# Batch 0's loads reordered, a third PSUM pair for its KV sums, an MLP bank taken early, and the last output tile in column halves: a change to a fused attention and MLP kernel

## The chip, the cores and the metric

The kernel runs on one core of one Trainium2 chip. The metric is the device time of one execution in microseconds (us), so lower is better. A chip has engines that run their own instruction streams: PE (TensorE, matmuls), PEld (its weight loads), DVE (VectorE), ACT (ScalarE), POOL (GpSimd) and SP (SyncE, which here only issues DMAs). "Span" below is the time from the first to the last instruction in one profiled execution; it is about 2 us less than the device time of the same execution.

A run is called slow where it is over 1.5% above the fastest of the same kernel, and fast otherwise. Ratios below are the mean time of one kernel's fast runs over that of the other's fast runs of the same rounds on the same chip, so they are not quite the ratio of the medians that are quoted beside them. The interval after a ratio is a 95% interval. "Faster" and "slower" mean by over 2%.

## The reference

Attention with random features (8 batches, 8 heads, 576 tokens, 64 dimensions, 128 features) feeds an MLP (4608 tokens, 512 to 2048 to 512).

```python
def _attn_ref(q, k, v, omega):
    scale = 1.0 / np.sqrt(np.sqrt(D))
    q_s, k_s = (q * scale, k * scale)
    def phi(x):
        proj = np.einsum('bhsd,md->bhsm', x, omega)
        h = proj - np.sum(x * x, axis=-1, keepdims=True) / 2.0
        h = h - np.max(h, axis=-1, keepdims=True)
        return np.exp(h) / np.sqrt(m)
    q_p, k_p = (phi(q_s), phi(k_s))
    kv = np.einsum('bhsm,bhsd->bhmd', k_p, v)
    z = np.sum(k_p, axis=2)
    num = np.einsum('bhsm,bhmd->bhsd', q_p, kv)
    den = np.einsum('bhsm,bhm->bhs', q_p, z)[..., None] + 1e-06
    return num / den

def _moe_ref(x, w_in, w_out):          # x: attention's output, 4608 x 512
    h = x @ w_in
    g = h * (1.0 / (1.0 + np.exp(-1.702 * h)))
    return g @ w_out
```

## The kernel before

The work is cut into 32 pairs of heads (4 to a batch) and 9 MLP blocks of 512 tokens. A pair passes through these steps; the names are those of the code.

- `ld`: k, q and v of the pair are loaded on POOL's DMA queue.
- `TK`, `TQ` (pairs 0 to 11, on PE) or `TD` (pairs 12 to 31, a DMA transpose on SP's queue, `qkT<-qk` in the profile): q and k are transposed.
- `K`, `Q` (PE) and `expK`, `expQ`, `expM` (ACT): projections and exponentials. `mx0`, `mx1`, `rec` (DVE) and `vp` (POOL or DVE) scale v.
- `KV` (PE), `kvs` (ACT), `ND` (PE), `rd` and `xm` (DVE): the KV sums, numerator and denominator, and their quotient.
- `X` and `evX` (pairs 0 to 7, PE and a copy) or `XD` (pairs 8 to 31, a DMA transpose on SP's queue, `xt<-xb`): the result is transposed for the MLP.

The MLP is `m1` (PE), `tanh` (ACT), `stt` (DVE), `m2` (PE), `store` (ACT) and `st` (output DMAs on SP's queue). MLP blocks start when their batches are done, so most of the attention runs in among the MLP's matmuls.

No instruction order is written out by hand: when the kernel is built, a list scheduler written in the kernel simulates all engines with a table of assumed durations, and emits each engine's instructions in the order that this simulation gives. Each engine's queue then runs strictly in that order, whatever the real durations are.

```python
ENGINES = {"K": {"P": 0.280}, "expK": {"A": 0.905}, "m1": {"P": 0.864}, ...
           "vp": {"G": 1.300, "D": 0.740}, "ld": {"G": 0.550},
           "TD": {"S": 2.1}, "XD": {"S": 1.2}, "st": {"S": 1.0}}          # G is POOL, S is SP
LOADS = [("k", 1), ("q", 1), ("k", 2), ("v", 1), ("q", 2), ("k", 3), ("v", 2), ("q", 3), ("v", 3)]
LOADS += [("wi", j) for j in range(4)]
...
    def kv_bank(o):                          # where a pair's KV sums go
        b = {"nd": nd["free"]}
        if o[1] < 4 and ("Q", 3) not in left:
            b["pq0"] = banks["pq"]["pq0"]
        return min(((t, x) for x, t in b.items() if t is not None), default=None)
...
            if st["m"] == 0:                 # the first MLP matmul waits for all of batch 0's banks
                if any(("Q", i) in left for i in range(4)):
                    return None
                t = max([t, banks["tr"]["tr1"], banks["pq"]["pq1"]])
...
        if kind == "ld":
            size = 2.90 if x[0] in ("wi", "wo") else 0.95      # assumed us of transfer
...
        def TD(i):
            t = qkp.tile([128, NS, 128], BF16, name="qkT", tag="qkT")
            nc.sync.dma_start_transpose(t[:], qk_t[i][:])
...
        def load_v(i, eng=nc.sync):
            t = stv.tile([128, NS, D], F32, name="v", tag="v")
            eng.dma_start(t[:], vv[i])
...
        for n, (o, eng) in enumerate(schedule(res)):
            emit(o, eng)
```

The softmax here doesn't subtract the row's maximum and nothing guards it: scores larger than these inputs give would overflow.

## Time and profile before

| | before |
|---|---|
| device time, median of 3 runs | 330.55 us (330.18 to 331.05) |
| span of the profiled execution | 535.4 us |
| granted PE clock in it | 0.559 |
| PE busy in it | 517.9 us, 97% |

The profiled execution and the timed ones are not in the same condition: the span is 1.6 times the time, because the PE clock that was granted was 0.559 of full speed. The page of the kernel before says so. Its first lines are the span and the busy time of each engine (us, share, instructions); the row PEclk gives the granted clock in tenths for 40 equal slices of the span; the last line divides the chain of work that ended last by engine.

```profile
span 535.4 us, 6610 instructions
PE 517.9 (97%) x2551; PEld 204.8 (38%) x2598; DVE 185.7 (35%) x342; ACT 196.3 (37%) x355; POOL 92.4 (17%) x161
...
PEclk7555555555555555555555555555555555555555
...
PE 95%; issue 2%; ACT 1%; DMA 1%; DVE 1%; SPq 0%; ACTq 0%
```

PE is 95% of the chain. In the timeline of the head (start in us, duration, engine, line, operation, tiles and shapes; in brackets the idle time before it and what ended it) the gaps that the change aims at are to be seen.

```profile
22.77 0.53 PE L528 MATMUL pqk<-vp,ke 64*128 64x65 bf16 x18
24.69 0.22 DVE L555 RECIPROCAL r<-pqk 128x10 f32<-128x10 f32 x1 [2.08 <-PE pqk L546]
26.98 0.65 ACT L435 ACTIVATE xt<-tr 128x576 bf16<-128x576 bf16 x1 [2.19 <-PE tr L573]
28.59 1.58 ACT L594 ACTIVATE th<-mo 128x512 bf16<-128x512 f32 x3 [0.95 <-PE mo L584]
```

Pair 3's KV sums start at 22.77 us, DVE stands idle for 2.08 us before it can go on, the last X copy of batch 0 starts at 26.98 us, and the first tanh of the MLP at 28.59 us.

SP's queue is where a reader would later have wished to look. In its timeline (start, time that the issue took, queue, line, operation, tiles, count) the first transposes of q and k of the kernel before stand at these times.

```profile
85.96 2.91 SPq L412 DMA_TRANSPOSE qkT<-qk  x2
94.91 1.24 SPq L412 DMA_TRANSPOSE qkT<-qk  x1
```

They are issued in 1.2 to 1.5 us each, and PE waits for none: the view of PE's waits (engine, tile and line, what it waited for, us in total, times, longest) has no line with `DMA qkT<-qk`. Its largest is this one.

```profile
PE mo L604 <- issue: 3.0, 13, 0.3
```

### The profile page before, as it was taken

How to read it: one execution, taken by the hardware profiler on the slowest of the kernel's cores; microseconds unless marked ns; L12 is line 12 of the kernel's file. 1: busy time of each engine (PE TensorE's matmuls, PEld its weight loads, DVE VectorE, ACT ScalarE, POOL GpSimd, SP SyncE). 2: the span in 40 equal slices, each digit the busy share in tenths (PEclk: the TensorE clock that was granted, in tenths of full speed). 3: DMA queues.
4: the chain of work that ended last, by engine and by line, in shares of the span. 5: the costliest groups of instructions: out<-in, count | busy, mean ns of one | idle time of the engine just before them, and what ended most of it. 6: DMA issues, size and time to landing. Idle time of an engine off the chain costs nothing.

```text
span 535.4 us, 6610 instructions
## 1 busy us (share of the span) xinstructions
PE 517.9 (97%) x2551; PEld 204.8 (38%) x2598; DVE 185.7 (35%) x342; ACT 196.3 (37%) x355; POOL 92.4 (17%) x161
## 2 busy tenths in 40 slices
PE   7999999999999999999999999999999999999996
PEld 3534344443443333434334333433333333333332
DVE  4655534643433423333333333323222222222200
ACT  5555525544543424343343333443222222222210
POOL 7527012333322212222112010000000000000000
PEclk7555555555555555555555555555555555555555
DMA  9999218466655353543355223211100001100011
GB/s 226 228 229 203 54 39 151 94 122 112 126 108 120 77 111 80 105 99 72 69 90 122 55 43 66 44 32 32 32 21 20 20 20 33 27 20 20 21 39 39
DMA packets 61807, 43.10 MB, mean 81 GB/s; under 512 B 42768, under 2 KB 54800, under 8 KB 61776
## 3 DMA queue, kind: packets, MB, share of 16 engines
q0 software_dynamic: 15632, 22.49, 21.5%
q1 hardware_dynamic: 46144, 20.20, 18.0%
q8 instruction: 20, 0.33, 0.3%
q14 instruction: 11, 0.09, 0.1%
HBM read 36.73 MB, written 9.44 MB: 86 GB/s over the span
## 4 chain that ended last, share of the span: by engine, by line
PE 95%; issue 2%; ACT 1%; DMA 1%; DVE 1%; SPq 0%; ACTq 0%
PE mo L584 41%; PE mo L604 40%; PE nd L546 3%; PE nd L528 3%; PE pqk L455 2%; PE pqk L484 2%; PE tr L423 1%; DMA qf<-in_q_dram 1%; PE tr L573 1%; PE tr L429 1%; PE tr L644 1%; PE nd L460 1%; DVE gT L598 1%; ACT th L594 0%; PE pq L484 0%
## 5 line engine op out<-in xcount | busy, mean ns | idle before, releaser
L584 PE MATMUL mo<-xt,win 128*128 128x512 bf16 x553 | 238.9, 577 | 4.4 <-issue 1.9
L604 PE MATMUL mo<-wout,gT 128*128 128x512 bf16 x555 | 238.3, 579 | 4.2 <-issue 3.0
L598 DVE SCALAR_TENSOR_TENSOR gT<-th,mo 128x512 bf16<-128x512 bf16 x144 | 98.7, 687 | 245.5 <-ACT th L594 245.4
L594 ACT ACTIVATE th<-mo 128x512 bf16<-128x512 f32 x144 | 85.8, 597 | 228.6 <-PE mo L584 219.4
L604 PEld LDWEIGHTS <-gT 128*128 128x128 bf16 x576 | 71.6, 129 | 127.8 <-issue 125.2
L584 PEld LDWEIGHTS <-win 128*128 128x128 bf16 x576 | 71.2, 129 | 126.1 <-issue 123.4
L516 POOL CAST vp<-em 128x9 bf16<-128x9 f32 x27 | 6.1, 225 | 260.4 <-DVE em L508 180.2
L617 ACT ACTIVATE osb<-mo 128x512 f32<-128x512 f32 x36 | 21.5, 597 | 46.9 <-PE mo L604 44.8
L473 ACT ACTIVATE ke<-pqk 128x1024 bf16<-128x1024 f32 x32 | 33.1, 1034 | 0.0
L493 ACT ACTIVATE qe<-pqk 128x1024 bf16<-128x1024 f32 x28 | 28.6, 1020 | 8.9 <-PE pqk L484 8.7
L517 POOL TENSOR_TENSOR vp<-v,em 128x576 bf16<-128x576 f32 x27 | 31.3, 1159 | 0.0
L546 PEld LDWEIGHTS <-qe 128*128 128x128 bf16 x320 | 20.6, 119 | 13.7 <-issue 10.9
L563 DVE TENSOR_TENSOR xb<-nd,r 128x640 bf16<-128x640 f32 x30 | 24.7, 823 | 0.9
L503 DVE TENSOR_REDUCE m<-hm 128x9 f32<-128x576 bf16 x32 | 24.0, 750 | 0.5
L528 PEld LDWEIGHTS <-ke 64*128 64x128 bf16 x576 | 16.2, 108 | 12.1 <-issue 5.2
L555 DVE RECIPROCAL r<-nd 128x10 f32<-128x10 f32 x30 | 6.5, 218 | 41.2 <-PE nd L546 23.1
L546 PE MATMUL nd<-kvs,qe 128*128 128x65 bf16 x300 | 20.5, 231 | 0.3
L394 POOL DMA_DIRECT2D v<-in_v_dram x31 | 18.2, 587 | 3.2 <-DMA qk<-in_q_dram 2.1
L499 DVE TENSOR_TENSOR hm<-ke 128x576 bf16<-128x576 bf16 x32 | 14.9, 466 | 10.7 <-ACT ke L473 10.7
L528 PE MATMUL nd<-vp,ke 64*128 64x65 bf16 x540 | 18.5, 222 | 0.0
L387 POOL DMA_DIRECT2D qk<-in_k_dram x31 | 17.2, 555 | 4.2 <-issue 1.7
L390 POOL DMA_DIRECT2D qk<-in_q_dram x31 | 17.1, 551 | 2.4 <-DMA win<-in_moe_w_in_dram 2.0
(55 smaller groups left out, 186.1 us busy)
## 6 DMA issues: line engine op xcount, KB each, us to landing
out_dram<-osb SPq DMA_DIRECT2D x72, 128.0 KB, 2.3
v<-in_v_dram POOLq DMA_DIRECT2D x31, 288.0 KB, 3.9
qk<-in_k_dram POOLq DMA_DIRECT2D x31, 144.0 KB, 4.1
qk<-in_q_dram POOLq DMA_DIRECT2D x31, 144.0 KB, 4.5
win<-in_moe_w_in_dram POOLq DMA_DIRECT2D x4, 512.0 KB, 10.3
wout<-in_moe_w_out_dram POOLq DMA_DIRECT2D x4, 512.0 KB, 9.9
xt<-xb SPq DMA_TRANSPOSE x24, 2.6
qkT<-qk SPq DMA_TRANSPOSE x20, 3.2
```

The lines of the kernel that those rows point to most:

```text
L473: nc.scalar.activation(out=st[i]["ke"][:, 1:9, :].rearrange("p (j e) f -> p e j f", e=2), in_=pk[:].rearrange("p e (j f) -> p e j f", f=12 ...
L493: nc.scalar.activation(out=dst, in_=src, func=AF.Exp, scale=SCALE)
L503: nc.vector.reduce_max(out=m[:], in_=st[i]["hm"][:], axis=AX.X)
L517: e.tensor_tensor(out=t[:, :, 0:64], in0=v_t[i][:], in1=em[:].unsqueeze(2).to_broadcast([128, NS, 64]), op=ALU.mult,)
L528: nc.tensor.matmul(nd[:, e, 0:65], lhsT=ke[64 * e : 64 * e + 64, s, :], rhs=t[64 * e : 64 * e + 64, s, :], start=(s == 0), stop=(s == NS - 1),
L546: nc.tensor.matmul(nd[:, e, g * 65 : (g + 1) * 65], lhsT=qe[i % NQE][:, e, g * 128 : (g + 1) * 128], rhs=t[:, e, :],)
L563: nc.vector.tensor_tensor(out=xb[:].rearrange("p g e d -> p e g d"), in0=v4[:, :, :, 0:64], in1=r[:].unsqueeze(3).to_broadcast([128, 2, NG ...
L584: nc.tensor.matmul(dst, lhsT=win[:, c, f * 128 : (f + 1) * 128], rhs=xt[c][:, n * 512 : (n + 1) * 512], start=(c == 0), stop=(c == NC_ - 1),)
L594: nc.scalar.activation(out=t[:], in_=src, func=AF.Tanh, scale=0.851)
L598: nc.vector.scalar_tensor_tensor(out=gts[n][:, f, :], in0=t[:], scalar=1.0, in1=src, op0=ALU.add, op1=ALU.mult)
L604: nc.tensor.matmul(dst, lhsT=gts[n][:, f, r * 128 : (r + 1) * 128], rhs=wout[:, f, :], start=(f == 0), stop=(f == NFC - 1),)
L617: nc.scalar.activation(out=o[:], in_=src, func=AF.Copy, scale=0.5)
```

## The change

The intent is to start the dense MLP earlier and to end it earlier.

- k and q of pairs 1 to 3 are loaded ahead of all v, and the transposes of a pair depend on free q/k buffers instead of on the KV sums three pairs back.
- KV sums of batch 0 may use a third PSUM pair, `pq1`, as well.
- The MLP's first bank is the second transpose bank, `tr1`; the other two are cut out of `pq1` when pair 3 is done. So only two groups, not three, begin in parts.
- The last output tile is computed, stored and sent in two halves of 256 columns.
- `vp` of pairs 0 and 3 is bound to DVE and of pairs 1 and 2 to POOL, and two of the scheduler's assumed transfer times are lowered.

```diff
-LOADS = [("k", 1), ("q", 1), ("k", 2), ("v", 1), ("q", 2), ("k", 3), ("v", 2), ("q", 3), ("v", 3)]
+LOADS = [("k", 1), ("q", 1), ("k", 2), ("q", 2), ("k", 3), ("q", 3), ("v", 1), ("v", 2), ("v", 3)]
...
+TILES = [4] * (NBLK - 1) + [5]
+def last(n, r):
+    return n == NBLK - 1 and r >= 3
...
-        deps["TK", i] = p("TK", i - 1) + p("KV", i - 3) + p("Q", i - 3) + l("k") + l("q")
+        deps["TK", i] = p("TK", i - 1) + p("K", i - NQK) + p("Q", i - NQK) + l("k") + l("q")
...
-            b["pq0"] = banks["pq"]["pq0"]
+            b.update({x: banks["pq"][x] for x in ("pq0", "pq1") if x in banks["pq"]})
...
+    def mo_bank():
+        b = dict(mob)
+        if "tr1" in banks["tr"]:
+            b["tr1"] = None if any(("X", i) in left for i in range(4)) else banks["tr"]["tr1"]
+        if "pq1" in banks["pq"]:
+            b["pq1"] = None if ("xm", 3) in left else banks["pq"]["pq1"]
+        return min(((t, x) for x, t in b.items() if t is not None), default=None)
...
-        if kind == "vp" and e == "D" and o[1] >= EARLY:
+        if kind == "vp" and e != ("D" if o[1] in (0, 3) else "G") and (o[1] < 4 or e == "D" and o[1] >= EARLY):
             return None
...
-            size = 2.90 if x[0] in ("wi", "wo") else 0.95
+            size = 2.65 if x[0] in ("wi", "wo") else 0.92
...
+        def cols(n, r):
+            return slice((r - 3) * 256, (r - 2) * 256) if last(n, r) else slice(0, DM)
...
         def send(n, r):
-                nc.sync.dma_start(ov[b, SLOT[rank]], o[64 * h : 64 * h + 64, :])
+                eng = nc.scalar if r == 4 and h else nc.sync
+                eng.dma_start(ov[b, SLOT[rank]][:, w], o[64 * h : 64 * h + 64, w])
```

On POOL's queue and on SP's (`st` are output stores):

```
POOL before: ... ldk13 ldq13 vp8   ldv13 ...
POOL after:  ... ldk13 vp8   ldq13 ldv13 ldk14 ldq14 vp9 ldv14 ldk15 ldq15 vp10 ...
SP before:   st0.0 st0.1 st0.2 TD12 TD13 XD8 TD14 XD9 XD10 TD15 XD11 st0.3 ...
SP after:    st0.0 st0.1 TD12 st0.2 XD8 TD13 XD9 TD14 XD10 XD11 TD15 XD12 st0.3 ...
```

More of the change, by code (lines that the diff above doesn't have):

```diff
@@ L128, in schedule @@
     a[0] = (
-        [("m1", 0, f, c) for f in range(3) for c in range(3)]
-        + [("m1", 0, f, 3) for f in range(3)]
-        + [("m1", 0, f, "all") for f in range(3, NFC)]
+        [("m1", 0, f, c) for f in range(2) for c in range(3)]
+        + [("m1", 0, f, 3) for f in range(2)]
+        + [("m1", 0, f, "all") for f in range(2, NFC)]
     )
-    bb = {n: [("m2", n, r, g) for r in range(4) for g in range(4)] for n in range(NBLK)}
+    bb = {n: [("m2", n, r, g) for r in range(TILES[n]) for g in range(4)] for n in range(NBLK)}
     m1s = sum((a[n] for n in range(NBLK)), [])
@@ L174, in schedule @@
     banks = {"tr": {"tr0": 0.0, "tr1": 0.0}, "pq": {"pq0": 0.0, "pq1": 0.0}}
-    mob = {"mo0": 0.0, "mo1": 0.0, "mo2": 0.0}
+    mob = {}
     landed = []
@@ L184, in kv_bank, with take_mo @@
         if o[1] < 4 and ("Q", 3) not in left:
-            b["pq0"] = banks["pq"]["pq0"]
+            b.update({x: banks["pq"][x] for x in ("pq0", "pq1") if x in banks["pq"]})
         return min(((t, x) for x, t in b.items() if t is not None), default=None)
+    def mo_bank():
[5 more added lines that the diff above has]
+        return min(((t, x) for x, t in b.items() if t is not None), default=None)
+    def take_mo(name, t):
+        if name == "tr1":
+            banks["tr"].pop("tr1")
+            name = "mo0"
+        if name == "pq1":
+            banks["pq"].pop("pq1")
+            mob["mo2"] = t
+            name = "mo1"
+        mob[name] = None
+        return name
     def when(o, e):
@@ L200, in when @@
                 return None
-            if st["m"] == 0:
-                if any(x is None for x in banks["tr"].values()) or any(x is None for x in banks["pq"].values()):
-                    return None
-                if any(("Q", i) in left for i in range(4)):
-                    return None
-                t = max([t, banks["tr"]["tr1"], banks["pq"]["pq1"]])
-            if o[3] in ("all", 0):
-                fr = [x for x in mob.values() if x is not None]
-                if not fr:
-                    return None
-                t = max(t, min(fr))
+            if o[3] in ("all", 0):
+                b = mo_bank()
+                if b is None:
+                    return None
+                t = max(t, b[0])
         if kind in ("ck", "cq"):
@@ L260, in schedule @@
         if kind in ("m1", "m2"):
-            dur = 0.864 if kind == "m2" or o[3] == "all" else 0.216
+            dur = 0.216 if kind == "m1" and o[3] != "all" else 0.432 if kind == "m2" and last(*o[1:3]) else 0.864
         if e == "P" and (kind in TILED) != st["tiled"]:
@@ L309, in schedule @@
         if kind in ("m1", "m2"):
-            if st["m"] == 0:
-                banks["tr"].pop("tr1")
-                banks["pq"].pop("pq1")
             st["m"] += 1
@@ L315, in schedule @@
             if o[3] in ("all", 0):
-                name = min((x for x in mob if mob[x] is not None), key=lambda x: mob[x])
-                res[o[:3]] = name
-                mob[name] = None
+                res[o[:3]] = take_mo(mo_bank()[1], start)
         if kind == "stt":
@@ L379 @@
         nd = psum.tile([128, 2, 512], F32, name="nd")
-        trB = psum1.tile([128, 1024], BF16, name="trB")
+        trB = psum.tile([128, 1024], BF16, name="trB")
         pq2 = psum1.tile([128, 2, 512], F32, name="pq2")
@@ L600, in stt @@
             )
+        def cols(n, r):
+            return slice((r - 3) * 256, (r - 2) * 256) if last(n, r) else slice(0, DM)
         def m2(n, r, quarter, dst):
+            w = cols(n, r)
+            dst = dst[:, 0 : w.stop - w.start]
+            m = min(r, 3)
             for f in range(4 * quarter, 4 * quarter + 4):
@@ L605, in m2 @@
                     dst,
-                    lhsT=gts[n][:, f, r * 128 : (r + 1) * 128],
-                    rhs=wout[:, f, :],
+                    lhsT=gts[n][:, f, m * 128 : (m + 1) * 128],
+                    rhs=wout[:, f, w],
                     start=(f == 0),
@@ L616, in store @@
             osb[n, r] = o
-            nc.scalar.activation(out=o[:], in_=src, func=AF.Copy, scale=0.5)
+            w = cols(n, r)
+            nc.scalar.activation(out=o[:, w], in_=src[:, 0 : w.stop - w.start], func=AF.Copy, scale=0.5)
         def send(n, r):
             o = osb.pop((n, r))
-            u = 2 * (4 * n + r)
+            u, w = 2 * (4 * n + min(r, 3)), cols(n, r)
             for h in range(2):
                 b, rank = divmod(u + h, NS)
-                nc.sync.dma_start(ov[b, SLOT[rank]], o[64 * h : 64 * h + 64, :])
+                eng = nc.scalar if r == 4 and h else nc.sync
+                eng.dma_start(ov[b, SLOT[rank]][:, w], o[64 * h : 64 * h + 64, w])
         nc.sync.dma_start(om_f[:], omega[:, :])
@@ L646 @@
         banks = {"tr0": tr, "tr1": trB, "pq0": pqk, "pq1": pq2, "nd": nd}
-        mo, ths = {}, {}
+        mo, ths = {"mo0": trB[:].bitcast(F32)}, {}
         def emit(o, eng):
             kind, a = o[0], o[1:]
-            if kind in ("m1", "m2") and not mo:
+            if kind == "m1" and res[o[:3]] != "mo0" and len(mo) == 1:
                 first.close()
                 p2 = ctx.enter_context(tc.tile_pool(name="psum2", bufs=1, space=bass.MemoryType.PSUM))
-                mo.update((f"mo{i}", p2.tile([128, 512], F32, name=f"mo{i}")) for i in range(3))
-                del banks["tr1"], banks["pq1"]
+                mo.update((f"mo{i}", p2.tile([128, 512], F32, name=f"mo{i}")[:]) for i in (1, 2))
+                del banks["pq1"]
             if kind == "idle":
@@ L666, in emit @@
                     gts[a[0]] = gtp.tile([128, NFC, 512], BF16, name="gT", tag="gT")
-                m1(a[0], a[1], mo[res[o[:3]]][:], range(4) if a[2] == "all" else [a[2]])
+                m1(a[0], a[1], mo[res[o[:3]]], range(4) if a[2] == "all" else [a[2]])
             elif kind == "tanh":
-                ths[a] = tanh(*a, mo[res[("m1",) + a]][:])
+                ths[a] = tanh(*a, mo[res[("m1",) + a]])
             elif kind == "stt":
-                stt(*a, ths.pop(a), mo[res[("m1",) + a]][:])
+                stt(*a, ths.pop(a), mo[res[("m1",) + a]])
             elif kind == "m2":
-                m2(*a, mo[res[o[:3]]][:])
+                m2(*a, mo[res[o[:3]]])
             elif kind == "store":
-                store(*a, mo[res[("m2",) + a]][:])
+                store(*a, mo[res[("m2",) + a]])
             elif kind in ("TK", "TQ", "X"):
```

## The prediction

> **What bounds the kernel now.** The profile was taken at a granted clock of 0.559 (span 535.4 us, timed 330.55), so I read DMA, VectorE (DVE) and ScalarE (ACT) durations from it, not the span. By the chain of waits PE is 95% of the span, 81% of it the two MLP matmul lines: once the MLP is dense, only removed PE work or PE waits count. By the Trainium skill, "TensorE: Matmul & The Clock Gate", Back-to-back issue gap, 512 columns take N/2.4 + 2.5 ns = 216 ns, so the 1152 MLP matmuls are about 249 us at full clock (an estimate; this profile shows 383 ns spacing). The change can gain in the head and the tail.
>
> **Head, from the timeline.** ACT is nearly full from 8.4 us (first exponentials) to 18.7 us (expQ of pair 3); DVE has hardly a gap from 15.0 to 22.6 us. The change leaves their work alone. Pair 3's scaled v is ready at 20.88 us, but its KV sums start only at 22.77: they need the pair bank pq0, which pair 1's xm frees at 21.87, and X1 stands before them on PE. So DVE sits 2.1 us waiting for ND3 (22.6 to 24.7), the last X copy ends at 27.63, the first tanh starts at 28.59, and PE waits again to 29.96 for a free MLP bank.
>
> With the change KV3 takes pq1 (free after expQ3, 18.7 us), so it starts at about 21, ND3 ends near 22.5, and DVE goes on to rd3 and xm3 without the wait. Loads: q3 lands at 11.8 us and v1 at 8.9; reordered, about 10.4 and 11.1, before v1's reciprocal (13.6). Transposes of pair 3 leave the path, but K3 still needs KV0 and ACT is full, so I give the load order under 0.5 us. vp0 moves to DVE, vp1 to POOL: even.
> Last X copy: 27.6 -> about 24.8 us. But the first-layer groups now begin after X3, which gives back six matmuls (1.3 us at full speed, partly behind the copy). Fourth group's start (the steady MLP): about 2.5 us earlier, estimate 1.5 to 3.
>
> **Tail.** Last matmul ends 530.88, ACT store 0.60, two DMA issues on SP 1.11, transfer of 256 KB until about 534.1, end 535.4: 4.5 us. Half columns: the ACT store about 0.4 (0.60 at 512 columns, 0.31 at 130), issues on SP and ACT in parallel, half the bytes: about 0.9 us saved. The extra half-width matmuls cost about 0.1.
>
> **Middle.** PE's order in the first blocks is reshuffled, same work: +-1 us.
>
> **Prediction:** 330.55 - 2.5 - 0.9 = 327.1 us, range 325.0 to 329.4 (8 in 10). Faster by over 2% 0.04, within 2% 0.95, slower by over 2% 0.01.
>
> **What would show it.** In the timeline: KV3 writing the second pair bank near 21 us; DVE's wait before rd3 gone; last X copy near 24.8 instead of 27.6 us; first tanh near 26 instead of 28.6; ACT's end of expQ3 unmoved (18 to 19 us). At the end, last matmul to span end 3.5 instead of 4.5 us.
>
> **What would make it wrong.** Pair 3's exponentials really move earlier (more gain); vp1 and vp2 now back to back on POOL delaying KV2 or lengthening DVE's max (it took 0.98 instead of 0.45 us beside POOL's vp2); a new bank wait in the MLP's first blocks that gives the head's gain back; the profile's slow clock hiding what is critical at full clock.

## The result, and the profile after

| | runs, us | median |
|---|---|---|
| before, same rounds | 330.55, 330.18, 331.05, 331.09 | 330.8 |
| after | 343.31, 343.69, 346.41 fast, 354.52 slow | 345.05 |

The ratio of the fast runs is 1.0416 (1.0349 to 1.0483): the changed kernel is slower by over 2%. The prediction said 327.1 us and gave that outcome a chance of 0.01.

The page after, with the same rows as before:

```profile
span 341.5 us, 6695 instructions
PE 319.9 (94%) x2618; PEld 157.1 (46%) x2618; DVE 180.7 (53%) x343; ACT 192.9 (56%) x355; POOL 92.1 (27%) x161
...
PEclk9999999997889999999999999999999999999999
...
PE 84%; DMA 11%; ACT 2%; DVE 1%; SPq 0%; issue 0%; ACTq 0%
```

This execution had the full clock, except in slices 10 to 12, and DMA is now 11% of the chain. The view of PE's waits and PE's timeline of the changed kernel name the wait.

```profile
PE pqk L470 <- DMA qkT<-qk: 12.7, 4, 6.8
```

```profile
85.43 0.61 PE L470 MATMUL pqk<-omT,qkT 64*128 64x128 bf16 x8 [6.85 <-DMA qkT<-qk]
94.77 0.40 PE L470 MATMUL pqk<-omT,qkT 64*128 64x128 bf16 x8 [2.73 <-DMA qkT<-qk]
```

PE waits 12.7 us in all for DMA transposes of q and k, 6.85 us of it at one place. The two waits shown, 9.6 us together, stand before K of pairs 13 and 14. The other two (1.66 and 1.45 us) stand before pairs 20 and 27; waits of that kind are found in the kernel before and in the repaired one too (below). The head, on the other hand, went as predicted. Its timeline after:

```profile
20.60 0.47 PE L543 MATMUL pq<-vp,ke 64*128 64x65 bf16 x18
22.24 0.21 DVE L570 RECIPROCAL r<-pq 128x10 f32<-128x10 f32 x1
23.86 0.65 ACT L450 ACTIVATE xt<-trB 128x576 bf16<-128x576 bf16 x1 [0.34 <-PE trB L588]
25.37 1.08 ACT L609 ACTIVATE th<-mo 128x512 bf16<-128x512 f32 x2 [0.86 <-PE mo L599]
26.74 1.02 PE L599 MATMUL mo<-xt,win 128*128 128x512 bf16 x4
```

KV3 starts at 20.60 us in the new bank, DVE has no gap before pair 3's reciprocal, the last X copy ends at 23.86 + 0.65 = 24.51 us, and the first tanh starts at 25.37 us.

### The profile page after: what moved, and what is told of

Read it like the earlier page. It is cut to its first block, busy times and chain, and to the rows that moved or that the text cites. A ratio compares the mean times of both kernels' runs of the same rounds, so it can differ in the third digit from the quotient of the medians.

```text
span 341.5 us, 6695 instructions
## 1 busy us (share of the span) xinstructions
PE 319.9 (94%) x2618; PEld 157.1 (46%) x2618; DVE 180.7 (53%) x343; ACT 192.9 (56%) x355; POOL 92.1 (27%) x161
## 3 DMA queue, kind: packets, MB, share of 16 engines
q1 hardware_dynamic: 46224, 20.13, 33.3%
## 4 chain that ended last, share of the span: by engine, by line
PE 84%; DMA 11%; ACT 2%; DVE 1%; SPq 0%; issue 0%; ACTq 0%
PE mo L599 26%; PE mo L625 18%; PE trB L625 17%; DMA qkT<-qk 10%; PE trB L599 9%; PE pqk L470 3%; PE nd L543 2%; PE nd L561 2%; PE pqk L499 2%; DMA qf<-in_q_dram 1%; PE tr L438 1%; PE tr L444 1%; ACT ke L488 1%; ACT qe L508 1%; DVE xb L578 0%; PE nd L475 0%
## 5 line engine op out<-in xcount | busy, mean ns | idle before, releaser
L613 DVE SCALAR_TENSOR_TENSOR gT<-th,mo 128x512 bf16<-128x512 bf16 x107 | 72.7, 682 | 71.8 <-ACT th L609 71.5
L599 PE MATMUL mo<-xt,win 128*128 128x512 bf16 x428 | 110.7, 383 | 0.0
L609 ACT ACTIVATE th<-mo 128x512 bf16<-128x512 f32 x107 | 64.0, 599 | 58.3 <-PE mo L599 57.8
L625 PEld LDWEIGHTS <-gT 128*128 128x128 bf16 x592 | 56.0, 99 | 62.2 <-issue 2.4
L599 PEld LDWEIGHTS <-win 128*128 128x128 bf16 x576 | 53.3, 98 | 61.6 <-issue 2.7
L625 PE MATMUL mo<-wout,gT 128*128 128x512 bf16 (+1 forms) x304 | 74.3, 374 | 0.0
L625 PE MATMUL trB<-wout,gT 128*128 128x512 bf16 (+1 forms) x288 | 72.7, 379 | 0.0
L599 PE MATMUL trB<-xt,win 128*128 128x512 bf16 x148 | 38.0, 379 | 0.0
L613 DVE SCALAR_TENSOR_TENSOR gT<-th,trB 128x512 bf16<-128x512 bf16 x37 | 25.2, 682 | 22.2 <-ACT th L609 22.0
L609 ACT ACTIVATE th<-trB 128x512 bf16<-128x512 f32 x37 | 22.2, 601 | 25.8 <-PE trB L599 25.6
L470 PE MATMUL pqk<-omT,qkT 64*128 64x128 bf16 x256 | 13.1, 224 | 12.7 <-DMA qkT<-qk 12.7
L479 ACT ACTIVATE ke<-nd 128x128 bf16<-128x128 f32 x32 | 8.9, 277 | 25.0 <-PE nd L476 15.5
L402 POOL DMA_DIRECT2D qk<-in_k_dram x31 | 16.9, 545 | 6.8 <-issue 2.1
```

The costliest lines, as they stand in the source:

```text
L402: nc.gpsimd.dma_start(qk_t[i][:, S : 2 * S], kv[i])
L470: nc.tensor.matmul(pk[:, e, j * 128 : (j + 1) * 128], lhsT=t[64 * e : 64 * e + 64, k0 + j, :], rhs=omT[64 * e : 64 * e + 64, :],)
L599: nc.tensor.matmul(dst, lhsT=win[:, c, f * 128 : (f + 1) * 128], rhs=xt[c][:, n * 512 : (n + 1) * 512], start=(c == 0), stop=(c == NC_ - 1),)
L609: nc.scalar.activation(out=t[:], in_=src, func=AF.Tanh, scale=0.851)
L613: nc.vector.scalar_tensor_tensor(out=gts[n][:, f, :], in0=t[:], scalar=1.0, in1=src, op0=ALU.add, op1=ALU.mult)
L625: nc.tensor.matmul(dst, lhsT=gts[n][:, f, m * 128 : (m + 1) * 128], rhs=wout[:, f, w], start=(f == 0), stop=(f == NFC - 1),)
```

## The experiments

The result suggested a theory and three rivals.

- Theory A: SP's queue. The X transpose `XD8` now stands ahead of `TD13`, and so on, so the q/k transposes come late by their place in the queue.
- Rival B: contention. The transposes run beside a burst of loads from POOL's queue and are slow for that reason, wherever they stand.
- Rival C: only the two assumed transfer times did it, by the order that they produce.
- Rival D: the new head or tail itself (its banks, its loads, its split tile) costs the time.

The recorded expectations use the letters A and B in another way. Their theory A covers the order on both queues, the late q load among it, and the loads that leave beside the transposes. Their theory B says that the DMA engines are full at full clock, whatever the order. Below, the letters mean the four items of this list unless the recorded ones are named.

The kernel before ran again in each set of rounds, so every ratio has its own runs of it on the same chip. "Landing" of a transpose is worked out from the trace's semaphore records: a transpose signals once from each of 16 DMA engines, and the tables count to the last signal. Expectations written earlier count to the first signal, so they say 18.1 us where the tables say 20.5. K of a pair is the first PE work that needs its transpose; its start is that of its first matmul.

### e0_before: a profile of the kernel before at full clock

The edit: none.

> The kernel before, unchanged, for a profile at a full clock (the only one so far had a clock of 0.559). All theories: about 330.5 us. Theory A (queue order: the change makes the q/k transposes of pairs 13 to 15 stand behind X transposes and behind a late q load, and they reach the DMA engines together with the loads): here these transposes take 1.2 to 2 us each on SP and PE waits less than 3 us for them between 60 and 100 us, against 12.7 us in the changed kernel. Theory B (the DMA engines are simply full at full clock once the head is shorter): the same transposes take 4 us and more here too, and PE waits for them, only less. Last X copy of batch 0 later than the changed kernel's 24.5 us by about 2.5 us, in both.

This execution took 335.75 us, somewhat long beside the seven runs of the same program in that set (331.24 to 334.42), at a mean clock of 0.992. It gives what the given profile could not. Its head timeline:

```profile
22.17 0.46 PE L528 MATMUL pqk<-vp,ke 64*128 64x65 bf16 x18
25.49 0.65 ACT L435 ACTIVATE xt<-tr 128x576 bf16<-128x576 bf16 x1 [1.39 <-PE tr L573]
26.60 1.57 ACT L594 ACTIVATE th<-mo 128x512 bf16<-128x512 f32 x3 [0.46 <-PE mo L584]
27.97 1.02 PE L584 MATMUL mo<-xt,win 128*128 128x512 bf16 x4 [0.97 <-DVE gT L598]
```

At full clock the head of the kernel before was already shorter: the first tanh is at 26.60, not 28.59 us, and the fourth MLP group at 27.97 us against 26.74 us after. So the head can gain about 1.2 us, not 2.5 us. And its line of PE's waits for transposes:

```profile
PE pqk L455 <- DMA qkT<-qk: 4.6, 2, 2.5
```

There are two waits at full clock in the kernel before as well, before K of pairs 19 and 26, at 121.6 and 183.4 us. Between 60 and 100 us there is none, and the transposes of pairs 12 to 15 are issued in 1.28 to 2.78 us each: between what the recorded A and B had expected. The last X copy ends at 26.14 us, 1.6 us after the changed kernel's, where 2.5 us had been expected. How near the transposes come to their deadlines is in this table; "slack" is the difference.

| pair | before, profile given (clock 0.559): landing, K after issue | before, full clock | after |
|---|---|---|---|
| 12 | 3.5, 23.8 us | 8.3, 12.6 us | 11.4, 14.9 us |
| 13 | 6.2, 30.3 us | 8.4, 15.8 us | 20.5, 20.5 us |
| 14 | 3.2, 32.5 us | 8.8, 16.6 us | 18.9, 19.0 us |
| 15 | 3.2, 22.1 us | 3.7, 12.3 us | 10.7, 10.8 us |

At the slow clock a transpose had about 19 us of slack or more. At full clock the kernel before has 4.3 to 8.6 us of it. After the change pairs 13, 14 and 15 have none: K starts within 0.2 us of the last signal. K's start after issue is itself stretched there, because K waited.

### e1_dma_constants_back: the changed kernel with the old transfer constants

```diff
-            size = 2.65 if x[0] in ("wi", "wo") else 0.92
+            size = 2.90 if x[0] in ("wi", "wo") else 0.95
```

> The changed kernel with only the two load sizes in the scheduler's own model put back (2.90 and 0.95 instead of 2.65 and 0.92): no data path differs, only the order that the scheduler picks (TD13 stands before XD8 again, the pairs 8 to 11 are less bunched). Theory A: 327 to 331 us, the waits for qkT mostly gone. Theory B: still above 340 us.

Measured: 336.19, 333.58, 336.0, 335.12 us, ratio 1.0099 (1.0043 to 1.0154). That is between the kernels. PE's waits for `qkT` fall from 12.7 to 4.9 us, so two assumed numbers (0.03 us a load, 0.25 us a weight block), which alter nothing but the emitted order, move the kernel by some 9 us. None of e1's waits stands before pairs 12 to 15; they are before pairs 18, 19 and 26. Rival C is part of it, but it only says that the order matters, not how. It missed the expected 327 to 331: this order also makes a worse head. Its fourth tanh came 21.21 us after the first exponential, where the changed kernel has 18.87 us, and a maximum on DVE took 1.36 us while POOL ran `vp` beside it.

### e2_sp_order, e3_sp_pool_order, e4_pool_order: the order on two queues

The changed kernel's order is kept, and only what differs on SP's queue around pairs 13 to 15 (e2), on POOL's queue around pair 13's q (e4), or both (e3) is put back. PE's order is untouched.

```diff
-        for n, (o, eng) in enumerate(schedule(res)):
+        ops = schedule(res)
+        x = next(y for y in ops if y[0] == ("ld", "q", 13))                   # POOL: e3 and e4
+        ops.remove(x)
+        ops.insert(next(i for i, y in enumerate(ops) if y[0] == ("vp", 8)), x)
+        for late, early in ((("TD", 13), ("XD", 8)), (("TD", 14), ("XD", 9)), (("TD", 15), ("XD", 11))):
+            x = next(y for y in ops if y[0] == late)                          # SP: e2 and e3
+            ops.remove(x)
+            ops.insert(next(i for i, y in enumerate(ops) if y[0] == early), x)
+        for n, (o, eng) in enumerate(ops):
```

> The changed kernel with only the order of SP's queue changed: q/k transposes 13, 14, 15 one place ahead of the X transposes 8, 9, 11, as in the kernel before. PE, ACT, DVE and POOL orders untouched. Theory A: PE's 12.7 us of waits for qkT fall to under 6 us, time 330 to 338. Theory B: unchanged within 2 us, 342 to 346.

> As e2_sp_order, and the load of q13 issued ahead of the scaling of v8 in POOL's queue, as in the kernel before. Theory A: q13 lands some 6 us earlier, transpose 13 leaves before loads 14 and 15 are under way; waits for qkT under 3 us, 326 to 332 us. Theory B: 342 to 346 us.

> The changed kernel with only the POOL queue changed: the load of q13 ahead of the scaling of v8; SP's order stays the changed one. It completes the square with e2 and e3. If the late q13 load is the trigger, 328 to 334 us; if both queues have to be right, 338 to 346 us. Theory B (DMA engines full whatever the order): 342 to 346 us, which e3 already speaks against.

| | runs, us | ratio to before | PE's wait for `qkT` |
|---|---|---|---|
| after | 343.31, 343.69, 346.41 | 1.0416 | 12.7 us |
| e2, SP's order back | 349.14, 350.58, 350.82 (slow: 359.18) | 1.0565 (1.0492 to 1.0637) | 9.6 us |
| e3, SP's and POOL's order back | 330.89, 332.21, 331.08, 332.37 | 0.9991 (0.9942 to 1.0039) | 2.5 us |
| e4, POOL's order back | 330.62, 331.44; 344.43, 346.79 | none taken | 3.6 us in a good run |

e2 was expected to win back most of the loss. It lost more: PE waits less for `qkT` but now also for an X transpose that has moved back. Its lines of PE's waits:

```profile
PE pqk L470 <- DMA qkT<-qk: 9.6, 5, 3.9
PE mo L599 <- DMA xt<-xb: 4.3, 1, 4.3
```

Its clock is also halved for longer, 17 us of the stretch from 81 to 110 us where the changed kernel has 10 us. So the order on SP's queue is not the cause by itself, and theory A of the list fell with it. e3, which also sends one load (pair 13's q) ahead of `vp8` on POOL's queue, brings back the whole loss. (By the recorded letters e3 speaks for A, 326 to 332 us, and against B, 342 to 346 us.) What is left of its waits is 2.5 us, before pairs 20 and 27:

```profile
PE pqk L470 <- DMA qkT<-qk: 2.5, 2, 1.3
```

Where the loss lies is shown by the windows view: window in us and its length, then busy us and instructions of PE, PEld, DVE, ACT and POOL, granted PE clock, DMA share, GB/s. The changed kernel:

```profile
70.00:80.00 10.00, 8.58 (x98) 4.38 (x98) 8.25 (x17) 7.42 (x15) 5.29 (x9) 1.00 1.18 150
80.00:90.00 10.00, 4.57 (x39) 1.98 (x40) 2.76 (x5) 2.23 (x6) 0.53 (x1) 0.66 1.28 96
90.00:100.00 10.00, 7.27 (x60) 3.23 (x59) 3.88 (x8) 5.09 (x10) 3.73 (x7) 0.83 1.31 177
```

And e3_sp_pool_order, the same windows:

```profile
70.00:80.00 10.00, 10.00 (x114) 5.17 (x113) 8.72 (x18) 8.39 (x18) 5.39 (x10) 1.00 1.39 139
80.00:90.00 10.00, 9.53 (x111) 4.76 (x110) 7.04 (x13) 7.17 (x14) 5.39 (x10) 1.00 1.24 207
90.00:100.00 10.00, 10.00 (x106) 4.99 (x105) 6.15 (x12) 7.06 (x15) 3.76 (x7) 1.00 1.23 209
```

The changed kernel's PE is idle 1.42 + 5.43 + 2.73 = 9.6 us in these 30 us, e3's 0.5 us. The granted clock falls to 0.66 and 0.83 as well: the trace's clock record has half the clock from 81.94 to 88.77 us and from 95.60 to 99.01 us. The first of these agrees with the Trainium skill, "TensorE: Matmul & The Clock Gate", section "What's actually happening", which says that an idle window of about 3.4 us halves the clock: the wait of 6.85 us is longer than that. The second follows a wait of only 2.73 us, so a shorter one was enough here. Other profiles go either way at such lengths: the clock was halved after PE had been idle for 2.06 us (e5) and 2.53 us (e0_before), and not after 2.54 us (e7) and 2.67 us (e1). The same is seen by milestones. The two kernels have the same order on PE, so the n-th tanh is the same work in both. Worked out from the trace, in us after the first exponential:

| | after | e3 | difference |
|---|---|---|---|
| 25th tanh | 63.53 | 63.53 | 0.00 |
| 33rd tanh | 91.40 | 79.16 | 12.24 |
| last instruction | 332.60 | 319.94 | 12.66 |

So 12.2 of the 12.7 us are lost between the 25th and the 33rd tanh. 9.6 - 0.5 = 9.1 us of that are PE's idle time. The rest fits the halved clock: PE was busy for 6.8 of the 10.2 us at half clock, which costs 3.4 us.

SP's queue shows what the transposes met. The changed kernel:

```profile
57.77 1.60 SPq L427 DMA_TRANSPOSE qkT<-qk  x1
...
63.30 1.44 SPq L433 DMA_TRANSPOSE xt<-xb  x1
64.91 7.10 SPq L427 DMA_TRANSPOSE qkT<-qk  x1
72.10 3.55 SPq L433 DMA_TRANSPOSE xt<-xb  x1
75.82 9.23 SPq L427 DMA_TRANSPOSE qkT<-qk  x1
...
90.57 4.06 SPq L427 DMA_TRANSPOSE qkT<-qk  x1
```

And e3_sp_pool_order:

```profile
58.01 1.56 SPq L427 DMA_TRANSPOSE qkT<-qk  x1
...
63.08 1.54 SPq L427 DMA_TRANSPOSE qkT<-qk  x1
64.72 1.47 SPq L433 DMA_TRANSPOSE xt<-xb  x1
66.36 2.59 SPq L427 DMA_TRANSPOSE qkT<-qk  x1
...
76.48 2.00 SPq L427 DMA_TRANSPOSE qkT<-qk  x1
```

In the changed kernel it takes 7.10 and 9.23 us only to issue pairs 13 and 14, and what stands behind them in the queue is issued only after that. What else was on the DMA engines comes from POOL. In the changed kernel POOL's `vp8` waits for DVE, and pair 13's q load stands behind it in the queue:

```profile
55.20 0.22 POOL L531 CAST vp<-em 128x9 bf16<-128x9 f32 x1 [5.77 <-DVE em L523]
...
56.45 0.59 POOL L405 DMA_DIRECT2D qk<-in_q_dram  x1
```

From 56.45 us on, seven loads leave within about 5 us, beside the transpose of pair 12 at 57.77 us. But the burst alone does not tell the two kernels apart. In e3 six of the same seven loads leave from 56.69 to 61.75 us, beside the transpose of pair 12 at 58.01 us, and it lands after 6.7 us instead of 11.4 us. What differs on POOL's queue is whether pair 13's q goes before the wait or at the head of the burst; how that slows the rest is not shown.

e4 says how thin the line is. The same program took 330.62 and 331.44 us in two runs and 344.43 and 346.79 us in two others, with the clock of the latter at 0.987 and 0.975. Those two are called slow, so no ratio is given. Their times are those of the changed kernel. The one profile is of a good run, so that the bad ones have the same collision is argued, not shown. The good run has the changed kernel's order on SP's queue, and its transposes of pairs 12 to 15 land in 6.6, 5.1, 4.1 and 4.4 us: in that run the order did no harm. In the square of the two queues, none of eight runs was at about 331 us with POOL's changed order (after, e2), two of four with only POOL's order put back (e4), and four of four with both (e3). So POOL's order decides most, and whether SP's order matters beside it is left open by two bad runs. e4 ran on another chip than e2 and e3, which is a second difference.

### e5_fewer_v_loads and e10_fewer_loads: the changed kernel with traffic taken away

Is it the loads that hold the transposes up, or their place in the order? Here the order is the changed kernel's, and only traffic is dropped. The results are wrong: pairs 14 to 18 use a constant tile instead of their v (e5), or of their k, q and v (e10).

```diff
         def load_v(i, eng=nc.sync):
+            if 14 <= i <= 18:
+                if i == 14:
+                    v_t[i] = const.tile([128, NS, D], F32, name="vfix")
+                    nc.gpsimd.memset(v_t[i][:], 0.05)
+                v_t[i] = v_t[14]
+                return
```

> Wrong result on purpose: the changed kernel with the loads of v14 to v18 left out (a constant tile is used; one POOL memset of about the time of a DMA issue replaces the first), all orders and waits otherwise those of the changed kernel. It takes away half of the written load bytes that run beside the transposes of 60 to 95 us. If the transposes are slow because loads run beside them (contention), transposes 13 and 14 take under 3 us each instead of 7.1 and 9.2, PE's waits for qkT fall from 12.7 to under 4 us, time 327 to 334. If what makes them late is only the order in the queues (they start late), they stay late and the time stays above 339 us.

> Wrong result on purpose: e5 with the k and q loads of pairs 14 to 18 left out too (constant tiles), orders otherwise those of the changed kernel, q13 still late. Contention: with nearly no load beside them, transposes 13 to 15 land in 3 to 6 us after their issue (18.1, 18.6 and 8.8 us in the changed kernel, 13.7, 12.6 and 7.6 in e5), PE's waits for qkT fall under 3 us, 328 to 331 us. If lateness in the queues alone were the cause they would still land after more than 10 us and the time would stay at e5's 332 or above.

| | landing of pairs 12, 13, 14, 15, us | PE's wait for `qkT` | runs, us |
|---|---|---|---|
| after | 11.4, 20.5, 18.9, 10.7 | 12.7 us | 343.31, 343.69, 346.41 |
| e5 | 13.8, 13.9, 12.9, 8.5 | 6.3 us | 334.58, 330.48, 329.73 (slow: 335.15) |
| e10 | 6.9, 3.3, 3.2, 4.3 | 2.3 us | 329.64, 333.07, 330.91 (slow: 336.88) |

The ratios are 1.0011 (0.994 to 1.0082) for e5 and 1.0033 (0.9987 to 1.0079) for e10. e5 missed what was expected of its landings and waits: the issues of pairs 13 and 14 still took 5.08 and 5.35 us, and PE waited 6.3 us instead of under 4 us (its profile is of the slow run at 335.15 us). Most of the time came back nevertheless, and with the k and q loads gone too the transposes land in about 3 to 7 us. The order of the queues is that of the changed kernel in both, and pairs 12 and 13, whose own k and q are loaded as ever, are issued at nearly the same times (57.3 and 64.2 us in e10, 57.8 and 64.9 us in the changed kernel). SP's queue in e10 and the line of PE's waits, of which none stands before pairs 12 to 15:

```profile
57.27 1.55 SPq L441 DMA_TRANSPOSE qkT<-qk  x1
...
64.19 1.28 SPq L441 DMA_TRANSPOSE qkT<-qk  x1
```

```profile
PE pqk L484 <- DMA qkT<-qk: 2.3, 3, 1.0
```

So the core of rival B is shown: at the same places in the queue, the transposes are late only when the loads run beside them. The loads are not enough by themselves, as e3 and e4's good run have them all. One rest of doubt is chance: the changed kernel itself was not run again beside e5 and e10, and e4, run on the same chip as these, had two good runs of four. All eight runs of e5 and e10 stayed under 337 us.

### e6_before_tail: the kernel before with the tail of the change

The edit is the hunks of TILES, last, cols, m2, store and send of the change, with the scheduler's assumed duration of a half tile, and nothing else.

> The kernel before with only the last output tile in column halves. By the two profiles at full clock, last matmul to end of span is 4.4 us before and 4.0 us after, less 0.1 us for the extra half-width matmuls: 0.3 us faster, 330.2 to 331.0 beside 331.3. The recorded prediction said 0.8 to 0.9.

Measured: 330.84, 329.99, 330.82, 330.32, 332.35, 332.59 us, ratio 0.9997 (0.9958 to 1.0037). The tail's gain is too small for the runs to resolve. In the traces it is half a microsecond. The tail of the kernel before at full clock (e0_before), from the last store to the span's end at 333.9 us, is 4.4 us:

```profile
329.48 0.60 ACT L617 ACTIVATE osb<-mo 128x512 f32<-128x512 f32 x1 [2.90 <-PE mo L604]
```

and that of the changed kernel, to 341.5 us, is 4.0 us, as it is in e6's own trace:

```profile
337.57 0.38 ACT L639 ACTIVATE osb<-trB 128x256 f32<-128x256 f32 x1 [1.36 <-PE trB L625]
337.98 0.56 ACTq L647 DMA_DIRECT2D out_dram<-osb  x1
```

### e7_head_tail_middle and e11_head_without_third_pair: the head and the tail without the new middle

This is the test of rival D. If the middle's order is what costs, the changed head and tail should gain on the kernel before once they are joined to its middle. e7 emits the changed schedule up to the first full MLP group, then the rest in the order of the kernel before, then the new tail.

```diff
+    n = next(n for n, (o, e) in enumerate(new) if o == ("m1", 0, 3, "all"))
+    head = new[:n]
+    rest = [x for x in old if x[0] not in done(head)]      # order of the kernel before
+    return head + rest + split_last_tile                   # sketch; PSUM bank names are set to fit
```

> The changed kernel's head (everything up to the fourth first-layer group) and its tail in halves, with the middle of all five engines in the order of the kernel before. If the loss sits wholly in the middle's order, this keeps the head's 1.2 us (fourth group starts at 26.7 instead of 28.0 us) and the tail's 0.3: 329.3 to 330.3 us, about 1.5 us under the kernel before, and PE's waits for qkT are under 3 us. If a shorter head by itself makes the middle's transfers collide, it ends over 335.

Measured: 332.64, 330.49, 329.87, 328.03, 330.72 us (slow: 334.33), median of all six 330.6, ratio 0.9973 (0.9923 to 1.0023). The loss is gone with the middle, so rival D falls; no gain is resolved either. Its profile still has 3.6 us of waits for `qkT`.

e11 is e7 without the third PSUM pair, one look.

```diff
-            b.update({x: banks["pq"][x] for x in ("pq0", "pq1") if x in banks["pq"]})
+            b["pq0"] = banks["pq"]["pq0"]
```

> e7 with the KV sums of batch 0 kept on pq0 and nd (no third pair); the other parts of the head are the changed kernel's. One look, only the head is read. If the third pair is what the head gains from, KV3 waits for pq0 again and the fourth first-layer group starts about 1.2 us later, counted from the first exponential; if the load order or the bank from trB makes the gain, it starts within 0.4 us of e7's.

It took 330.72 us. Its fourth tanh comes 20.35 us after the first exponential. In e7 it comes at 19.74 us, in the changed kernel and e3 at 18.87 us, and in all three profiles that have the old head (e0, e6, e13) at 20.18 us within 0.01 us. The seven other profiles that have the changed head with the third pair give 18.87 to 19.77 us (after, e2 to e5, e9, e10), so one head varies by 0.9 us from run to run, and e11 lies 0.6 us above all of them. In e11 KV3 starts 13.62 us after the first exponential, in e7 12.57 us. Together this speaks for the third pair as what the head gains from, though the 0.6 us lie between the two expectations and e11 is one run. The gain is between 0.4 and 1.3 us.

### e8_transposes_and_loads and e12_mixed_traffic: the traffic by itself

Both hold no attention or MLP. Their outputs are wrong, which doesn't matter for the times. e8 times six such transposes alone, the k, q and v loads of six pairs alone, and both at once.

```diff
+        def transposes():
+            for i in range(6):
+                nc.sync.dma_start_transpose(qkT[i][:], src[:])
+        def loads():
+            for i in range(6):
+                nc.gpsimd.dma_start(qk[i][:, S : 2 * S], kv[i])
+                nc.gpsimd.dma_start(qk[i][:, 0:S], qv[i])
+                nc.gpsimd.dma_start(vt[i][:], vv[i])
+        transposes(); fence(); loads(); fence(); loads(); transposes(); fence()      # all twice
```

> Wrong result on purpose: the disputed cost by itself. No MLP and no attention: twice in a row, with fences between the phases, (1) six q/k-sized DMA transposes from SP alone, (2) six pairs' k, q, v loads from POOL alone, (3) the same loads and the same six transposes at once. If transposes and loads only share the engines' time, phase 3 takes about the sum of phases 1 and 2 and a 256-byte transpose packet stays near the 20 to 30 ns of the good runs. If they disturb each other (the mean packet was 67 to 217 ns in the changed kernel's bad stretch), phase 3 takes over 1.3 times the sum, with mean transpose packets over 60 ns.

From the trace's DMA records (one execution, 143.11 us):

| e8 | takes |
|---|---|
| six transposes alone | 10.5 and 10.5 us; a landing every 1.4 us, each about 3.4 us after its issue; 256-byte packets of 21 ns |
| loads of six pairs alone | 17.6 and 17.5 us |
| both at once | 27.7 and 25.5 us |

These are the two passes, from the first issue to the last landing. Both at once take no longer than the sum, 28.1 us, where one theory had expected over 1.3 times the sum. So the mixture costs no throughput here. What it costs is latency. The loads of the mixture end after 23.7 and 21.5 us instead of 17.5, and the first four transposes land 9.3, 16.9, 17.5 and 12.7 us after their issue (8.0, 15.1, 17.3 and 12.4 us in the second pass), as two or three of them are under way at once, and the second and third land 4.6 to 9.7 us after the one before. Between 54 and 66 us the engines pass 1280 transpose packets and 1156 load packets, about 1.1 to 1, and a transpose has 1152 packets of 256 bytes, while a pair's loads have 320 of 1152 or 4608 bytes. This is what one would expect from the Trainium skill, "DMA: Bandwidth & Descriptors", section "Queues, rings and completion order", which says that each DMA engine goes round-robin between the queue rows that have work, packet by packet. It is not a test of it: the page's packet is about 9 to 17 descriptors, and whether a packet of these records is one of those the runs do not show.

So the plain mixture can by itself bring a transpose to 17 us, when others are under way before it. In the changed kernel they were: pair 13's was issued at 64.91 us, before pair 12's had landed (69.16 us). But there the packets themselves were longer as well. Between 60 and 98 us the 256-byte packets of the transposes took 18 ns in the middle but 120 ns at the 90th percentile, and the packets of v loads 191 ns in the middle and 1224 ns at the 90th percentile; in e3 the 90th percentiles were 20 and 359 ns. That does cost throughput: from 80 to 90 us the windows above have 96 GB/s in the changed kernel and 207 GB/s in e3, at nearly the same DMA share (1.28 and 1.24). e12 tried to find what brings this about: four phases with the same loads and six transposes each, with X transposes and with matmul, ACT and DVE work added by turns.

```diff
+        def transposes(x):
+            for i in range(6):
+                nc.sync.dma_start_transpose(qkT[i][:], src[:])
+                if x:
+                    nc.sync.dma_start_transpose(xt[i][:], xsrc[:])
+        for x, work in ((0, 0), (1, 0), (1, 1), (0, 1)):
+            loads(work); transposes(x); fence()
```

> Wrong result on purpose. Four fenced phases, each with six pairs' loads and six q/k transposes at once: (1) as e8, (2) with six X-sized transposes between them, (3) as 2 with matmuls, tanh, gating and a POOL multiply running, (4) as 1 with that work. If X transposes in the queue make the stretch, the 90th percentile of a 256-byte packet goes from about 30 ns in phase 1 to over 100 ns in 2 and 3; if the compute engines' work makes it, in 3 and 4; if neither, all four stay near 30 ns and the cause of the stretch stays open.

| e12, phase | first to last packet | 256-byte packets while loads run: mean, 90th percentile |
|---|---|---|
| 1: loads and transposes | 33.3 us | 62, 196 ns |
| 2: and X transposes | 33.0 us | 39, 31 ns |
| 3: and X transposes and compute | 36.4 us | 54, 192 ns |
| 4: and compute | 26.0 us | 32, 31 ns |

Phases 1 and 3 show long packets, phases 2 and 4 do not. Neither the X transposes nor the compute goes with it, and phase 1 is the plain mix of e8, which took 26.0 and 23.8 us there, counted in the same way. The long packets come in one stretch of a phase: from 37 to 51 us in phase 1 and from 114 to 122 us in phase 3 the engines move 46 to 118 GB/s, before and after mostly 150 to 280 GB/s. So the same traffic can fall in either of two modes, and what picks the mode stays open. With e4, whose one program took 331 and 345 us, it is the second sign of such a thing.

### e9_early_transposes and e13_before_early_transposes: transposes given more time

Where latency is the trouble, the cure is to issue the transposes earlier. This is tried on the later waits, of the kind before pairs 19 and 26; the transposes of pairs 12 to 15 stay where they are. e9 is e7 with the transposes of pairs 16 to 31 moved up in SP's queue to about 12 MLP units ahead of their K (their data allow it), and e13 does this to the kernel before, with the old head and tail.

```diff
+    for i in range(16, NPAIR):
+        m, at = 0, {}
+        for n, (o, e) in enumerate(ops):
+            m += o[0] in ("m1", "m2") and (o[0] == "m2" or o[3] == "all")
+            at[o] = (n, m)
+        x = ops.pop(at["TD", i][0])
+        first = max(at[d][0] for d in (("TD", i - 1), ("K", i - NQK), ("Q", i - NQK), ("ld", "k", i), ("ld", "q", i)))
+        want = min(n for n, y in at.values() if y >= at["K", i][1] - 12)
+        ops.insert(min(max(first + 1, want), at["TD", i][0]), x)
```

> e7 with the q/k transposes of pairs 16 to 31 moved ahead in SP's queue, to about 12 MLP units (10 us) ahead of their K matmuls instead of 5 to 8. In e7 and in the kernel before, the later transposes that collide with others land after 6 to 8 us and PE waits 1 to 2.6 us for them. If those waits make the run-to-run spread and hide the head's gain, PE's waits for qkT fall under 0.5 us and the time is 328.5 to 329.8 us with less spread; if earlier transposes just collide with more, 330 to 333.

> The kernel before with only the transposes of pairs 16 to 31 moved ahead in SP's queue, as in e9; its own head and tail. If e9's 2.2 us (328.9 beside 331.1) are head and tail 1.5 and the later transposes' waits 0.7, this gives 330.0 to 330.6 beside 331.1; if the transposes made most of it, 329.0 to 329.6.

| | runs, us | median | before, same rounds | ratio |
|---|---|---|---|---|
| e9 | 327.11, 327.75, 327.47, 331.06, 330.0, 330.67 | 328.88 | 331.06 | 0.9942 (0.990 to 0.9985) |
| e13 | 328.77, 330.37, 331.03, 329.43, 329.23, 328.6 | 329.33 | 331.46 | 0.9957 (0.992 to 0.9993) |

Neither profile has a wait for `qkT` any more. The first line of e9's view of PE's waits is one from the first microseconds:

```profile
PE tr L715 <- ACT qk L961: 1.6, 1, 1.6
```

In e9, K of pairs 16 to 31 comes 13.4 to 18.7 us after the issue, and the longest landing is 10.5 us. In e0 those were 4.8 to 9.4 and 9.0 us, so the kernel before was short of slack there as well. e9 is the fastest of all these kernels: 0.6% below the kernel before, and about 4.5% below the changed one (on another chip). Both intervals lie below 1, though well within 2%. As e13 gets nearly the same without the new head and tail, most of e9's gain comes from the earlier transposes. e9 and e13 are not told apart by these runs.

## Why the prediction was wrong, point by point

- **The step that failed:** "Middle. PE's order in the first blocks is reshuffled, same work: +-1 us." The work was the same, but the term measured at least 12.2 us, which is what the changed kernel loses to e3 between the 25th and the 33rd tanh. I looked at PE's order only. The orders on POOL's and SP's queues were reshuffled too, and both could have been compared before the prediction. With pair 13's q load moved behind a POOL wait of 5.77 us, the transposes of pairs 13 and 14 landed 20.5 and 18.9 us after their issue, and PE waited 9.6 us for them; with that load and SP's order put back (e3) they landed after 6.5 and 10.8 us, and PE did not wait for them.
- **"once the MLP is dense, only removed PE work or PE waits count"** held, but I took it that no new PE wait would come. Two came, of 6.85 and 2.73 us, and half the clock with each. (The other 3.1 of the 12.7 us are later waits such as e0 and e3 have too.)
- **What hid it:** the profile that I read had a clock of 0.559. There K of pairs 12 to 15 came 22 to 33 us after the issue of its transpose, at full clock 12.3 to 16.6 us. I knew of the slow clock and listed it as what could make the prediction wrong ("the profile's slow clock hiding what is critical at full clock"), yet still took DMA waits from that profile: that there was none. The transposes landed no sooner at full clock (3.7 to 8.8 us, against 3.2 to 6.2 us), but their deadlines came sooner. A profile at full clock would have shown this small slack and two later waits, though no wait in this stretch either: the order of the changed kernel had to be looked at as well.
- **Head:** the mechanism was right. KV3 in the second bank at 20.60 us (predicted about 21), DVE's wait gone, last X copy at 24.51 us (24.8), first tanh at 25.37 us (26), expQ3's end at 19.17 us (18 to 19). The size was wrong: 2.5 us predicted, 1.3 us measured to the fourth tanh (20.18 to 18.87 us; 0.4 us in e7), because the kernel before reached its first tanh at 26.60 us at full clock, and not at 28.59 us. Again it was the slow profile.
- **Tail:** right in kind; 0.5 us in the traces (4.4 to 4.0 us) for 0.9 predicted. The prediction counted from the end of the last matmul (4.5 to 3.5 us), these numbers from the start of the last store just behind it. The extra matmuls cost about 0.04 us: two halves of 1.79 and 1.75 us for one tile of 3.50 us.
- **PE at 216 ns a matmul:** the full-clock trace agrees. Groups of four start 0.86 us apart (300.67 and 301.53 us in e0), so 216 ns each.
- **The sum:** measured was +13.7 us (means of fast runs, 344.47 and 330.72 us). With -1.3 us for the head and -0.5 us for the tail, the middle would have cost 15.5 us against the kernel before, 3 us more than the 12.2 us against e3. e3, for its part, should be 1.8 us ahead of the kernel before and is level with it (0.9942 to 1.0039 as a ratio, so up to 1.9 us). Runs of one kernel spread by two to five microseconds and neither head nor tail was resolved end to end (e6, e7), so the sum closes only roughly.

What was shown: the loss lies in the wait for transposes between about 72 and 100 us (waits, windows, milestones), it goes when two queues get their old order with PE's order kept (e3), and it goes when the loads go with the changed order kept (e10). What stays open: how one load's place on POOL's queue brings on the bad stretch, when nearly the same burst of loads leaves in e3; why packets of both kinds stretch in one mode and not in the other under the same traffic (e12); and whether e4's bad runs are the same collision, as they were not profiled.

## What to carry to other kernels

Where an order comes from a scheduler, compare the order on every queue before and after, the DMA-issuing ones first, since a change in the head can rearrange loads and transposes far from it. For each DMA on which the critical engine depends, read the slack between its landing and its use at the clock of the timed runs, and scale it if the profile ran slower. Issue DMA transposes of small packets early enough to last through a burst of loads: here 13 to 19 us ahead removed the waits (e9, e13), where 5 to 9 us left them. That is no cover for the bad stretch of the changed kernel, where landings took up to 20.5 us.

## What the Trainium skill lacked or had wrong

- "DMA: Bandwidth & Descriptors", section "Rules for kernel authors", says "A transpose next to ordinary DMAs needs nothing". As to correctness no run here speaks against it. As to time it lacks the cost: a transpose that lands in 3.4 us by itself (e8) took 18.9 and 20.5 us beside the loads of the changed kernel, and 3.2 and 3.3 us with those loads dropped (e10).
- "DMA: Bandwidth & Descriptors", section "Queues, rings and completion order", has the round-robin by packets but not what follows for a transfer of many small packets: about 1.1 of its packets for one of the loads', so landings of up to 17.5 us instead of 3.4 us (e8), with no longer total time (27.7 and 25.5 us against 10.5 + 17.6).
- No page that I read has the two modes of such a mix: 256-byte packets with a 90th percentile of 196 ns in one phase and 31 ns in another (e12), and one program at 331 and 344 to 347 us (e4).
- "TensorE: Matmul & The Clock Gate", section "Back-to-back issue gap", gives about 131 ns for a matmul of 512 columns as the sustained spacing of a real kernel and calls its formula, 216 ns, that of a single one. In this kernel's dense stretch with a weight load before every matmul the spacing is 216 ns (four matmuls in 0.86 us), so the formula holds here and the other figure does not.
